# Alpha of the first nine units in ring ph, and one ScalarE sum over pc and rc

## The chip, the cores and the metric

The kernel runs on one NeuronCore of a Trainium2 chip. The metric is the time of one execution on the device in microseconds (us), as the median of several runs. The kernel before takes 537.9 us (three runs, 537.58 to 538.51).

A core has five engines that run side by side, each with its own queue of instructions in a fixed order: TensorE (PE in the profile, with PEld for the loads of its stationary operand), VectorE (DVE), ScalarE (ACT), GpSimd (POOL) and SyncE (SP), which here only starts the transfers (DMA). SBUF is the working memory with 128 partitions. PSUM takes TensorE's results; it has eight banks, each with room for 128 x 512 numbers of four bytes.

## The reference

First a gated linear attention runs over 768 steps for 4 batches, 8 heads and 48 numbers per head; then a feed-forward network with 2048 hidden numbers runs over the 3072 tokens.

```python
state = np.zeros((B, H, D, D))
for t in range(S):
    state = alpha[:, :, t, :, None] * state + einsum('bhd,bhe->bhde', k[:, :, t], v[:, :, t])
    y[:, :, t] = einsum('bhd,bhde->bhe', q[:, :, t], state)
x = y.transpose(0, 2, 1, 3).reshape(B * S, H * D)
h = x @ w_in
out = np.maximum(0.01 * h, h) @ w_out
```

B, H, S, D are 4, 8, 768, 48. All alphas lie between 0.8 and 1.

## The kernel before, in words

**Units.** The attention is cut into 24 units: 6 blocks of 128 tokens by 4 batches, block by block. Two heads lie above one another in the partitions (rows 0 to 47 and rows 64 to 111), so the 8 heads are 4 pairs. For a unit `scans` (line 330) makes `pc`, the running product of alpha along the tokens, and `rc`, its reciprocal, which is made from a reciprocal at every 16th token and one long scan from the end of the block to its start (line 342). `scaled_q` and `scaled_k` (356, 364) multiply q by `pc` and k by `rc`; `scores` (372) multiplies them on TensorE, for the even heads into one bank (`s` = 0) and for the odd heads into another (`s` = 1); `mask_scores` (381) copies both into SBUF and clears what lies after the diagonal; `k_tokens` (397) turns k back to tokens; `outputs` (407) makes the unit's output `y` (score tiles by values, line 423, and the old state by q, line 417) and the step `kv` of the state (k as tokens by values, line 434); `next_state` (447) adds it up. `sum_up` (350) sums `pc` and `rc` of the unit into `acc`; at the very end (line 646) the sums are compared with 2 to the 40th, and only if one is too large a slow exact path runs, which does not happen with these inputs.

**The output's two halves.** `y` is split into a high part `xh` (copied at line 440) and what is left, `xl`. In the first nine units TensorE subtracts `xh` in the bank of `y` itself (442) and ScalarE copies the rest (443), so `y` keeps its bank until then.

**Two ways of loading.** The first nine units (`AHEAD` = 9) are loaded with tokens in the partitions, and alpha, q and k are turned by TensorE, four transposes each, into a PSUM bank (line 302), from which VectorE works on. The later 15 units are loaded in pieces and turned by VectorE in SBUF (line 311); they take no bank for that.

**PSUM.** Ring `ph` (pool `ps_h`) has two banks, rings `a` and `b` (pool `ps_x`) three each; that is all eight. `bank()` (line 69) gives the banks of the first nine units in turn from a and b: the first call takes a, the next b, the next a, and so on. A unit makes eight calls, in the order of the program: the alpha of the next unit, its two score banks, the bank of `k_tokens`, q and k of the next unit, `y` and `kv`. Ring `ph` has the warm-up (`keep_warm`, line 188, which keeps TensorE at work with products that nobody reads), the weights 0 and 1 (lines 275 to 280), and the first product of each feed-forward item (line 515).

**Feed-forward.** The tokens of three units make a block of 384 columns, and there are 8 blocks. An item is one block and one of 16 slices of the hidden numbers: nine products into `ph` (519), the leaky maximum on ScalarE and VectorE (522 to 531), and, three items later, nine products into three banks that add up over the 16 slices (546), which are from ring b for block 0, from ring a for block 1 and from ring b for all later blocks. Blocks 0 and 1 run in turn while the weights come in: each slice arrives as 64-bit words and is made into a high and a low part by `converting` (239) on ScalarE and VectorE. From block 2 on the attention of units 9 to 23 is mixed in, a step at a time.

**Order.** The program is written down in the order of the generator `attention` (481): the scans of the next unit, then scores, mask, `k_tokens` and sum of this one, then q and k of the next, then output and state of this one. A planner that runs when the program is built follows the instructions in a model of the chip's times and gives each engine, among those whose inputs and whose bank or buffer are at hand, the one that stands first in the program; the order that comes out of it is the fixed order of each queue. `issue_after` (through `behind`, line 112) holds an instruction behind another in the same queue. `AFTER`, `BEGIN` and `STARTS` (573 to 577) are such places for the weights 0 to 2 and for the first two items.

**Buffers.** `pc` and `rc` are two tiles of [128, 4, 128] each, and each has two buffers, so the scans of a unit wait until nobody reads those of two units before. `idle`, the tile of the warm-up, is in ring ph.

Of the kernel before, what the change touches and what calls it, by code (L numbers as in the profile page):

```python
# [9 lines left out]
F32 = mybir.dt.float32  # L10
# [4 lines left out]
AF = mybir.ActivationFunctionType  # L15
# [7 lines left out]
def gated_linear_attn_ffn(ctx, tc, q, k, v, alpha, w_in, w_out, out):  # L23
    nc = tc.nc
    B, H, S, D = q.shape
    NT, DM = out.shape
    DF = w_in.shape[1]
    P = 128
    C = 128
    NC = S // C  # L30
    NP = H // 2
# [4 lines left out]
    BR = HB + D  # L36
# [3 lines left out]
    NU = len(units)  # L40
# [3 lines left out]
    cst = ctx.enter_context(tc.tile_pool(name="cst", bufs=1))  # L44
    fast = ctx.enter_context(ExitStack())
    atp = fast.enter_context(tc.tile_pool(name="atp", bufs=2))
    cvp = fast.enter_context(tc.tile_pool(name="cvp", bufs=2))
    ffp = fast.enter_context(tc.tile_pool(name="ffp", bufs=2))
    ps_h = fast.enter_context(tc.tile_pool(name="ps_h", bufs=2, space=bass.MemoryType.PSUM))
    ps_x = fast.enter_context(tc.tile_pool(name="ps_x", bufs=3, space=bass.MemoryType.PSUM))  # L50

    NL = 2, 2, 2
    NV = 3
# [4 lines left out]
    PITCH = RUN + GAP  # L58
# [10 lines left out]
    def bank(tag=None):  # L69
        if tag is None:  # L70
            tag = kinds[0]
            kinds.append(kinds.pop(0))
        return ps_x.tile([P, 512], F32, name=tag)

    def pieces(name, dtype, *shapes):

        sizes = [math.prod(shape) for shape in shapes]
        whole = cst.tile([P, sum(sizes)], dtype, name=name)
        parts = []
        for n, shape in enumerate(shapes):  # L80
            part = whole[:, sum(sizes[:n]):sum(sizes[:n + 1])]
            axes = "abc"[:len(shape)]
            if len(shape) > 1:
                part = part.rearrange(f"p ({' '.join(axes)}) -> p {' '.join(axes)}", **dict(zip(axes, shape)))
            parts.append(part)
        return parts

    ident, mask, ones, acc, seed, *rest = pieces(
        "small", F32, (P,), (C,), (1,), (2 * NU,), (NP, C), *[(NP, BR)] * B, *[(DM,)] * NV, *[(NP * PITCH,)] * sum(NL)
    )  # L90
    state, vals_sb, rest = rest[:B], rest[B:B + NV], rest[B + NV:]
    loads_sb = [[rest.pop(0) for _ in range(n)] for n in NL]
# [19 lines left out]
    def behind(*key):  # L112

        return tc.issue_after(made[key].ins) if key in made else nullcontext()
# [4 lines left out]
    def loaded(u, i):  # L119
        return places(u, i)[u % len(places(u, i))]  # L120

    def load_next(u, i):

        for n in range(u + 1, u + 3 + NS):
            if n < NU and n - len(places(n, i)) == u:
                load(n, i)

    def by_token(t):
        return t[:, 0:H * HB].rearrange("t (h d) -> t h d", h=H)
# [58 lines left out]
    def keep_warm(n):  # L188

        for _ in range(n):  # L190
            nc.tensor.matmul(idle[:, 0:C], seed[:, 0, :], seed[:, 1, :], start=True, stop=True)  # L191
# [101 lines left out]
    def banks4():  # L293
        return bank().rearrange("r (p n) -> r p n", p=NP)

    def transposed(u, i, name, **kw):

        src = loaded(u, i)
        if u < AHEAD:
            ps = banks4()  # L300
            for p in range(NP):
                last = nc.tensor.transpose(  # L302
                    ps[:, p, :], by_token(src)[:, 2 * p:2 * p + 2, :].rearrange("t h d -> t (h d)"), ident
                )
                if u == 0 and p % 2:
                    with tc.issue_after(last.ins):
                        keep_warm(2)
            return ps
        t = atp.tile([P, NP, C], F32, name=name, **kw)
        src = src.rearrange("r (p n) -> r p n", p=NP)[:, :, 0:RUN]  # L310
        nc.vector.transpose(  # L311
            t.rearrange("r p (j t) -> r p t j", t=T4),
            src.rearrange("r p (t d) -> r p t d", t=T4)[:, :, :, 0:32],
        )
        return t
# [4 lines left out]
    live, masked, sums, dense = {}, {}, {}, {}  # L320
# [6 lines left out]
    def every(t, first):  # L327
        return t.rearrange("r p (m s) -> r p m s", s=STEP)[:, :, :, first]

    def scans(u):  # L330
        aT = transposed(u, 0, "e", bufs=1)
        pc = atp.tile([P, NP, C], F32, name="pc")
        rc = atp.tile([P, NP, C], F32, name="rc")
        pe = atp.tile([P, NP, 1], F32, name="pe", bufs=3)
        for p in range(NP):
            nc.vector.tensor_tensor_scan(pc[:, p, :], aT[:, p, :], ones.broadcast_to([P, C]), 1.0, ALU.mult, ALU.mult)  # L336
        nc.vector.memset(every(aT, 0), 0.0)
        nc.vector.reciprocal(every(seed, STEP - 1), every(pc, STEP - 1))
        flat = [t.rearrange("r p t -> r (p t)") for t in (aT, seed, rc)]
        last = seed[:, NP - 1, C - 1:C]  # L340
        nc.gpsimd.tensor_copy(rc[:, NP - 1, C - 1:C], last)
        nc.vector.tensor_tensor_scan(  # L342
            flat[2][:, NP * C - 2::-1], flat[0][:, NP * C - 1:0:-1], flat[1][:, NP * C - 2::-1], last, ALU.mult, ALU.add
        )
        load_next(u, 0)
        nc.gpsimd.tensor_copy(pe, pc[:, :, C - 1:C])  # L346
        live[u] = [pc, rc, pe]
        sums[u] = pc, rc

    def sum_up(u):  # L350

        with behind("sm", u):
            for n, t in enumerate(sums.pop(u)):
                nc.scalar.activation(t, t, AF.Abs, accum_out=acc[:, 2 * u + n:2 * u + n + 1])

    def scaled_q(u):
        pc = live[u][0]
        qT = transposed(u, 1, "qs")
        load_next(u, 1)
        qs = qT if u >= AHEAD else atp.tile([P, NP, C], F32, name="qs")  # L360
        nc.vector.tensor_tensor(qs, qT, pc, ALU.mult)
        live[u].append(qs)

    def scaled_k(u):
        pc, rc, pe, qs = live[u]
        kT = transposed(u, 2, "ks")
        load_next(u, 2)
        ks = kT if u >= AHEAD else atp.tile([P, NP, C], F32, name="ks")
        made["ks", u] = nc.vector.tensor_tensor(ks, kT, rc, ALU.mult)  # L369
        live[u] = [pe, qs, ks]  # L370
# [110 lines left out]
    def attention(first, last):  # L481

        for u in range(first - 1, last):
            new, old = u + 1 < last, u >= first
            if new:
                scans(u + 1)
                yield
            if old:
                scores(u)
                yield  # L490
                mask_scores(u)
                yield
                k_tokens(u)
                sum_up(u)
                yield
            if new:
                scaled_q(u + 1)
                yield
                scaled_k(u + 1)
                yield  # L500
            if old:
                outputs(u)
                yield
                next_state(u)
                if u % UPB == UPB - 1:
                    gather(u // UPB)
                    ready.add(u // UPB)
                yield
# [71 lines left out]
    for n, _ in enumerate(st):  # L580
# [8 lines left out]
        u = AHEAD - EARLY + converted  # L589
# [4 lines left out]
        if n in STARTS:  # L594
            i, f = items[len(gs)][:2]
# [8 lines left out]
    for n in range(len(items) + LAG):  # L604
        slices = 0
        if n < len(items):
            i, f, slices, _ = items[n]
# [27 lines left out]
        for half in range(2):  # L635
# [5 lines left out]
            if half == 0 and n >= LAG:  # L641
                i, f, _, tag = items[n - LAG]
                ffn_out(i, f, gs.pop(n - LAG), tag)


    fine = cst.tile([P, 2 * NU], F32, name="fine")
    nc.vector.tensor_scalar(fine, acc, RANGE, None, ALU.is_lt)
    least = cst.tile([P, 1], F32, name="least")
    nc.vector.tensor_reduce(least, fine, mybir.AxisListType.X, ALU.min)
# [123 lines left out]
```

## Time and profile before

| | before |
|---|---|
| median of 3 runs | 537.9 us (537.58 to 538.51) |
| the profiled execution's own time | 538.98 us |
| its span in the profile | 537.2 us |
| granted TensorE clock, mean | 0.998 |
| busy PE / PEld / DVE / ACT / POOL | 98 / 94 / 69 / 44 / 11 % |
| instructions | 10028 |

Times in the profile are counted from the span's start. A row of a group names line, engine, operation, out<-in, the count, and the time of one; "idle before" is the time in which the engine had nothing to do just ahead of an instruction, and the name behind the arrow is what ended it. Ends of matmuls are modelled, so PE looks busy also where it does not run at its peak; starts are what the argument goes by. A product of four-byte numbers shows as two records, so the eight products of the scores are 16. "a" and "b" are the two rings, with the buffer's number left out.

In this profile the first nine units take the time to 66.75 us, where the first product of the feed-forward network starts. From there to 530 us TensorE works on the feed-forward network, with the attention of units 9 to 23 mixed in after 163 us.

### The profile page before, as it was taken

What the parts mean: (1) busy time and instruction counts of PE and PEld (TensorE: products, weight loads), DVE (VectorE), ACT (ScalarE), POOL (GpSimd) and SP (SyncE); (2) the same over time, 40 slices, a digit from 0 to 9 for tenths busy, and PEclk for the clock granted to TensorE, in tenths of its full rate; (3) what the DMA queues carried; (4) which work ended last, traced back from release to release, by engine and by line L of the source; (5) the groups of instructions that cost most, each with busy time, mean ns of one, the idle gap of its engine ahead of it and who ended that gap; (6) DMA issues with size and microseconds to landing.
All of it is one profiled execution on the core that took longest, in us unless ns stands there. A gap on an engine that the chain in (4) does not pass through costs nothing.

```text
span 537.2 us, 10028 instructions
## 1 busy us (share of the span) xinstructions
PE 528.6 (98%) x3807; PEld 507.3 (94%) x3807; DVE 370.8 (69%) x688; ACT 238.1 (44%) x502; POOL 59.4 (11%) x144
## 2 busy tenths in 40 slices
PE   8999999999999999999999999999999999999995
PEld 7888799999999999999999999999999999999995
DVE  7777579999999997786586685675786434333331
ACT  2667575555543544344334444335343344224331
POOL 5444210000000111101101101001010000000000
PEclk9999999999999999999999999999999999999999
DMA  9999936444835543542332432423201000001001
GB/s 146 164 205 173 231 79 133 118 119 120 194 70 147 157 97 84 103 96 72 70 88 58 114 76 49 92 54 87 70 4 35 21 26 1 22 1 45 1 1 49
DMA packets 92982, 46.64 MB, mean 87 GB/s; under 512 B 57856, under 2 KB 90112, under 8 KB 92928
## 3 DMA queue, kind: packets, MB, share of 16 engines
q1 hardware_dynamic: 92928, 45.93, 39.1%
q8 instruction: 32, 0.52, 0.5%
q14 instruction: 22, 0.18, 0.1%
HBM read 38.83 MB, written 4.72 MB: 81 GB/s over the span
## 4 chain that ended last, share of the span: by engine, by line
PE 97%; DVE 1%; issue 0%; ACT 0%; DVEq 0%
PE ph L519 38%; PE b L546 33%; PE a L546 5%; PE a L378 5%; PE a L423 3%; PE a L417 3%; PE b L423 2%; PE a L434 2%; PE a L402 2%; PE b L302 1%; PE b L378 1%; PE a L302 1%; PE ph L191 1%; PE b L417 1%; PE ph L277 1%; PE ph L279 1%
## 5 line engine op out<-in xcount | busy, mean ns | idle before, releaser
L519 PE MATMUL ph<-large,w 128*128 128x384 f32 x1152 | 225.3, 337 | 0.0
L519 PEld LDWEIGHTS ph<-large,w 128*128 128x128 f32 x1152 | 200.8, 188 | 1.1 <-PE a L423 0.2
L546 PE MATMUL b<-w,gh 128*128 128x384 f32 x672 | 168.8, 340 | 0.0
L525 DVE TENSOR_TENSOR t<-ph,t 128x384 f32<-128x384 f32 x128 | 70.2, 548 | 79.3 <-ACT t L522 79.1
L522 ACT ACTIVATE t<-ph 128x384 f32<-128x384 f32 x128 | 62.6, 490 | 135.5 <-PE ph L519 135.5
L546 PEld LDWEIGHTS b<-w,gh 128*128 128x128 f32 x672 | 119.4, 188 | 2.1 <-issue 0.4
L527 ACT CAST gh<-t 128x384 fp32r<-128x384 f32 x128 | 65.8, 514 | 108.8 <-DVE t L525 108.8
L546 PE MATMUL b<-w,gl 128*128 128x384 f32 x336 | 107.2, 335 | 0.0
L531 DVE TENSOR_TENSOR gl<-t,gh 128x384 fp32r<-128x384 f32 x128 | 70.2, 548 | 34.3 <-ACT gh L527 34.3
L546 PEld LDWEIGHTS b<-w,gl 128*128 128x128 f32 x336 | 62.6, 188 | 0.0
L389 POOL TENSOR_SCALAR_AFFINE_SELECT sm<-sm 128x512 f32<-128x512 f32 x33 | 20.6, 634 | 204.0 <-ACT sm L388 204.0
L378 PEld LDWEIGHTS a<-qs,ks 48*128 48x128 f32 x312 | 23.9, 187 | 5.5 <-issue 4.5
L378 PE MATMUL a<-qs,ks 48*128 48x128 f32 x312 | 28.6, 285 | 0.3 <-DVE ks L369 0.3
L311 DVE STREAM_TRANSPOSE ks<-small 128x512 f32<-128x512 f32 x15 | 16.6, 1117 | 14.3 <-PE a L402 14.3
L346 POOL COPY pe<-pc 128x4 f32<-128x4 f32 x24 | 5.0, 210 | 176.7 <-DVE pc L336 174.5
L395 POOL TENSOR_TENSOR small<-us,pe 48x192 f32<-48x192 f32 x40 | 20.5, 512 | 1.5
L388 ACT COPY sm<-a 128x512 f32<-128x512 f32 x24 | 14.0, 584 | 14.9 <-PE b L378 11.1
L336 DVE TENSOR_TENSOR_SCAN pc<-e,small 128x128 f32<-128x128 f32 x60 | 20.3, 397 | 0.0
L546 PE MATMUL a<-w,gh 128*128 128x384 f32 x96 | 19.3, 336 | 0.0
L342 DVE TENSOR_TENSOR_SCAN rc<-e,small 128x511 f32<-128x511 f32 x15 | 19.1, 1271 | 0.2
L423 PE MATMUL a<-sm,small 128*48 128x128 f32 x256 | 17.3, 277 | 0.0
L267 ACT CAST w<-bits 128x768 fp32r<-128x768 f32 x16 | 13.4, 841 | 8.0 <-DVE bits L264 8.0
(110 smaller groups left out, 563.9 us busy)
## 6 DMA issues: line engine op xcount, KB each, us to landing
raw<-in_moe_w_out_dram SPq DMA_DIRECT2D x16, 384.0 KB, 4.1
raw<-in_moe_w_in_dram SPq DMA_DIRECT2D x32, 144.0 KB, 4.0
out_dram<-o SPq DMA_DIRECT2D x24, 192.0 KB, 1.9
small<-in_v_dram SPq DMA_DIRECT2D x20, 192.0 KB, 3.3
small<-in_alpha_dram SPq DMA_DIRECT2D x32, 96.0 KB, 2.2
small<-in_q_dram SPq DMA_DIRECT2D x30, 96.0 KB, 2.3
small<-in_k_dram SPq DMA_DIRECT2D x30, 96.0 KB, 2.2
small<-in_alpha_dram SPq DMA_DIRECT2D x30, 80.0 KB, 2.2
```

The lines of the kernel that those rows point to most:

```text
L336: nc.vector.tensor_tensor_scan(pc[:, p, :], aT[:, p, :], ones.broadcast_to([P, C]), 1.0, ALU.mult, ALU.mult)
L378: nc.tensor.matmul(ss[s][:, p, :], ks[lo:lo + D, p, :], qs[lo:lo + D, p, :], start=True, stop=True)
L389: made["mask", u] = nc.gpsimd.affine_select(out=sm[s], in_=sm[s], compare_op=ALU.is_ge, fill=0.0, base=0, pattern=[[0, NP], [1, C]], chann ...
L395: nc.gpsimd.tensor_tensor(*scalings.pop(0))
L417: nc.tensor.matmul(y[0:BR, p, :], W[0:BR, p, :], qs[0:BR, p, :], start=p == 0, stop=False, skip_group_check=True)
L423: nc.tensor.matmul(y[lo:lo + m, p, :], V[:, c:c + m], masked[u][s][:, p, :], start=not tb and p == 0, stop=p == NP - 1, skip_group_check=True,
L519: nc.tensor.matmul(ph, w_in_of(f, wn, g), xt[:, g, :], start=n == 0, stop=n == 3 * NG - 1)
L522: put(ordered, "ACT", lambda: nc.scalar.mul(t, ph, 0.01))
L525: put(ordered, "DVE", lambda: nc.vector.tensor_tensor(t, ph, t, ALU.max))
L527: put(ordered, "ACT", lambda: nc.scalar.copy(gh, t))
L531: made["gl", i, f] = put(ordered, "DVE", lambda: nc.vector.tensor_tensor(gl, t, gh.bitcast(F32), ALU.subtract))
L546: product = nc.tensor.matmul(po[j], gt[:, js], w_out_of(f, wn), start=f == 0 and n == 0, stop=f == NF - 1 and n == 2)
```

## The change

In the first nine units the alpha of a unit is turned into a bank of ring ph and not into the next bank of a and b; q and k stay as they are. A unit so makes seven calls of `bank()`, and what had a bank of a in one unit has one of b in the next. `pc` and `rc` become the two halves of one tile with two buffers, and `sum_up` sums both in one ScalarE instruction over 1024 numbers a partition into one column of `acc`, which has 24 columns for 48; the comparison at the end is over 24 columns. The alternation for the rest of the kernel (`kinds[:] = "a"` ahead of the items) is unchanged.

```diff
-        "small", F32, (P,), (C,), (1,), (2 * NU,), (NP, C), *[(NP, BR)] * B, ...
+        "small", F32, (P,), (C,), (1,), (NU,), (NP, C), *[(NP, BR)] * B, ...
 ...
     def transposed(u, i, name, **kw):
         src = loaded(u, i)
         if u < AHEAD:
-            ps = banks4()
+            ps = banks4() if i else ps_h.tile([P, 512], F32, name="ph").rearrange("r (p n) -> r p n", p=NP)
 ...
     def scans(u):
         aT = transposed(u, 0, "e", bufs=1)
-        pc = atp.tile([P, NP, C], F32, name="pc")
-        rc = atp.tile([P, NP, C], F32, name="rc")
+        both = atp.tile([P, 2, NP, C], F32, name="pc")
+        pc, rc = both[:, 0], both[:, 1]
 ...
-        sums[u] = pc, rc
+        sums[u] = both
 
     def sum_up(u):
         with behind("sm", u):
-            for n, t in enumerate(sums.pop(u)):
-                nc.scalar.activation(t, t, AF.Abs, accum_out=acc[:, 2 * u + n:2 * u + n + 1])
+            t = sums.pop(u)
+            nc.scalar.activation(t, t, AF.Abs, accum_out=acc[:, u:u + 1])
 ...
-    fine = cst.tile([P, 2 * NU], F32, name="fine")
+    fine = cst.tile([P, NU], F32, name="fine")
```

`transposed` is called with `i` = 0 for alpha, 1 for q and 2 for k, so only alpha goes to ph.

More of the change, by code (lines that the diff above doesn't have):

```diff
@@ L88, in gated_linear_attn_ffn @@
     ident, mask, ones, acc, seed, *rest = pieces(
-        "small", F32, (P,), (C,), (1,), (2 * NU,), (NP, C), *[(NP, BR)] * B, *[(DM,)] * NV, *[(NP * PITCH,)] * sum(NL)
+        "small", F32, (P,), (C,), (1,), (NU,), (NP, C), *[(NP, BR)] * B, *[(DM,)] * NV, *[(NP * PITCH,)] * sum(NL)
     )
```

## The prediction

> **What bounds the kernel now.** I read first the page's chain of waits, to see which engine sets the end.
>
> ```profile
> PE 97%; DVE 1%; issue 0%; ACT 0%; DVEq 0%
> ```
>
> TensorE does, nearly everywhere: 97% of the chain is PE. What a change elsewhere saves counts only where it shortens PE's queue. The change touches the nine units before the feed-forward work and one ScalarE step of all 24 units, so next I cut the span into stages (window, PE busy, PEld busy, DVE busy, ACT busy, POOL busy, clock, DMA).
>
> ```profile
> 10.00:31.38 21.38, 21.04 (x257) 17.25 (x257) 17.32 (x37) 14.70 (x37) 10.38 (x25) 1.00 1.20 168
> 31.38:44.67 13.29, 13.29 (x147) 11.25 (x146) 9.51 (x21) 8.62 (x21) 6.02 (x14) 1.00 1.11 209
> 44.67:66.75 22.08, 21.66 (x191) 16.41 (x190) 14.12 (x28) 13.11 (x29) 7.04 (x12) 1.00 0.99 202
> 82.00:163.00 81.00, 81.00 (x468) 81.00 (x467) 81.00 (x132) 43.36 (x76) 0.28 (x1) 1.00 0.51 123
> ```
>
> From 10 to 66.75 us PE shows no idle time worth naming, yet the weight loads fill only 74 to 85% of it, against all of it later. So PE's queue is full but not efficient there. From 82 to 163 us PE and DVE are both full and start from the end of the first stage; what the first stage saves moves everything behind it forward. The first stage's length is therefore the question.
>
> **Where PE loses time in it.** A unit's scores are eight matrix products in two banks, `s` = 0 in rows 0 to 47, `s` = 1 in rows 64 to 111. The answers on line 378 (min/median/max ns, first and last start) for units 2 and 3:
>
> ```profile
> L378 PE MATMUL a<-qs,ks x8: 272/272/373, 20.4 to 21.3; 48*128 48x128 f32 x8
> L378 PE MATMUL b<-qs,ks x8: 272/272/373, 22.0 to 22.9; 48*128 48x128 f32 x8
> L378 PE MATMUL a<-qs,ks x8: 272/272/373, 27.1 to 27.9; 48*128 48x128 f32 x8
> L378 PE MATMUL b<-qs,ks x8: 272/272/373, 27.1 to 27.9; 48*128 48x128 f32 x8
> ```
>
> In unit 3 both halves run at once; in unit 2 one after the other, and each takes as long as the pair. Units 4 and 6 are torn in the same way; the second half of unit 6, and unit 4 in the time line of PE (start, us, what), which has the price:
>
> ```profile
> L378 PE MATMUL b<-qs,ks x8: 271/272/373, 47.1 to 48.0; 48*128 48x128 f32 x8
> 31.97 1.16 PE L378 MATMUL a<-qs,ks 48*128 48x128 f32 x8
> 33.05 0.60 PE L402 MATMUL a<-small,ks 112*128 112x112 f32 x4
> 33.58 1.16 PE L378 MATMUL b<-qs,ks 48*128 48x128 f32 x8
> ```
>
> From start to start a lone half takes 33.05 - 31.97 = 1.08 us. The order of PE's queue is fixed before the run, so this is the planner's order: it had bank a for one half and not yet bank b for the other. Such a unit also tears its products with the values apart (L434 into one bank, L423 into the other). Units 3 and 4:
>
> ```profile
> 29.79 0.32 PE L423 MATMUL b<-sm,spare 128*64 128x128 f32 x1
> 31.38 0.66 PE L302 MATMUL b<-small 128*128 128x128 f32 x4
> ...
> 35.49 0.67 PE L434 MATMUL a<-spare,ktok 128*64 128x48 f32 x16
> 36.09 0.66 PE L302 MATMUL b<-small 128*128 128x128 f32 x4
> ...
> 37.55 0.42 PE L423 MATMUL b<-sm,spare 128*48 128x128 f32 x2
> 37.90 0.66 PE L302 MATMUL b<-small 128*128 128x128 f32 x4
> 38.49 1.07 PE L423 MATMUL b<-sm,spare 128*48 128x128 f32 x14
> ```
>
> Interleaved (unit 3): 31.38 - 29.79 = 1.59 us for both. Torn (unit 4): 0.60 + 0.35 + 1.00, the last without the 0.07 us by which pieces overlap, = 1.95 us, so 0.36 more.
>
> **Why bank b is short.** The alternation gives b, in every unit, the next alpha, one score half, the next q and the output y. How long two of these hold it shows around unit 2:
>
> ```profile
> 18.21 0.32 PE L423 MATMUL b<-sm,small 128*64 128x128 f32 x1
> 19.80 0.66 PE L302 MATMUL b<-small,spare 128*128 128x128 f32 x4
> 22.43 1.28 DVE L342 TENSOR_TENSOR_SCAN rc<-b,small 128x511 f32<-128x511 f32 x1
> 24.30 0.60 ACT L443 CAST large<-b 112x512 fp32r<-112x512 f32 x1
> ```
>
> y of unit 1 from 18.21 to 24.90 is 6.7 us; alpha of unit 3 from 19.80 to the end of its backward scan at 23.71 is 3.9; together 10.6. An untorn unit needs about 5.0 us of PE, an estimate from the rows above: scores 1.08, y and kv 1.59, three transposes of 0.59 like that from 31.38 to 31.97, L402 0.53. In 5.0 us three banks offer 15, so 4.4 are left for a score half and for q, each of which is written, waits for its reader and is read. A ring so near to its limit makes the planner wait.
>
> **The change part by part.** *Alpha into ring ph.* In units 0 to 8 alpha leaves the a/b alternation: seven banks a unit instead of eight, so what took b takes a in the next unit, and y alternates. Of the 10.6 us of long holders each of the two rings then has half of y, 3.4 of its 15 us a unit, and ph has alpha, 3.9 of 10; no ring is near its limit. The number of matmuls and transposes is unchanged. If all three split units become whole: 3 x 1.08 = 3.24 us, plus 0.36 for unit 4 and the same, an estimate, for unit 2, which is torn likewise; unit 6's two pieces are each whole, so nothing there. Together 4.0 us. Bounds: 0 (the planner splits as before) to 4.0 from this alone. I take all of it, since the splits sit only where b is short, and no other ring limit is left.
>
> *What ph then meets.* Its first bank is the one the warm-up writes:
>
> ```profile
> 7.76 0.66 PE L302 MATMUL b<-small 128*128 128x128 f32 x4
> 8.25 1.95 PE L191 MATMUL ph<-small 128*128 128x128 f32 x16
> 10.40 1.35 DVE L336 TENSOR_TENSOR_SCAN pc<-b,small 128x128 f32<-128x128 f32 x4
> 48.95 1.27 DVE L342 TENSOR_TENSOR_SCAN rc<-b,small 128x511 f32<-128x511 f32 x1
> L277 PE MATMUL ph<-bits,small x8: 486/486/561, 48.7 to 59.7; 128*128 128x384 f32 x8
> ```
>
> Today alpha of unit 1 is transposed at 7.76, before the last warm-up; it will have to wait for the warm-up's end at about 10.1 or for unit 0's backward scan. That puts 0.59 us of transposes before the first scores, which began at 10.54, and DVE's scan of unit 1 some 0.4 later. Bounds 0 to 0.6; I take 0.2, since PE was idle just before the scores. Weights 0 and 1 pass through ph too (L277, from 48.7), where alpha of units 7 and 8 may hold a bank. PE would wait up to the 1.5 us from 48.7 to the end of unit 7's backward scan (48.95 + 1.27). I take 0: the first feed-forward product that needs these weights comes at 66.75 (next fence), and the units' own products can go ahead of them. Without that cover it is 1.5 for each of the two weights, most of the gain.
>
> *Banks at the end.* With 7 instead of 8 a unit, unit 8's y falls on b and the three output banks of the first feed-forward item (b) wait for its last reader. Rows:
>
> ```profile
> 66.75 3.42 PE L519 MATMUL ph<-large,w 128*128 128x384 f32 x18
> 73.88 0.86 PE L546 MATMUL b<-w,gh 128*128 128x384 f32 x4
> 75.00 0.59 ACT L443 CAST large<-a 112x512 fp32r<-112x512 f32 x1 [0.22 <-PE a L442]
> ```
>
> The third bank is wanted about 1.0 us after 73.88 and free at 75.6: 0 to 0.7 us, of which PE fills most with the next item (L519). I take 0.2.
>
> *The sums.* Two passes of 512 become one of 1024, with one accumulator read instead of two.
>
> ```profile
> L354 ACT ACTIVATE pc<-pc x24: 633/643/664, 13.1 to 448.1; 128x512 f32<-128x512 f32 x24
> 42.12 0.66 ACT L354 ACTIVATE pc<-pc 128x512 f32<-128x512 f32 x1
> 43.36 0.92 ACT L258 ACTIVATE raw<-raw 128x768 f32<-128x768 f32 x1
> 70.13 0.56 DVE L261 TENSOR_SCALAR bits<-raw 128x768 int32<-128x768 int32 x1 [7.64 <-ACT raw L258]
> ```
>
> The old pair takes 43.36 - 42.12 = 1.24 us from start to start, 0.62 each with its accumulator read, 0.02 under the 643 ns of the pass itself. From 643 at 512 to 920 at 768 is 1.08 ns an element, so 1024 takes 1.20, less the 0.02: 1.18. The saving is 0.06 us a unit (bounds, from a pass that scales with its length to one whose length is free: -0.1 to 0.6) and lies under PE's work in all units but unit 8, whose sum stands ahead of L258, on which DVE's work from 70.13 waits; I take 0.1 there. The price is a wait: both scans now write one tile, so a unit's first scan waits for the whole sum of two units before, not for its first half. The Trainium skill, "ScalarE: Activation LUTs", section "What ACT_TABLE_LOAD costs", gives 186 ns + 0.833 ns an element and an overlap of 93 ns: 1.04 us at 1024 and a saving of 0.2; its 613 ns at 512 is 5% under the row here, and the difference lies under PE by either.
>
> *Sum:* -4.0 + 0.2 + 0.2 - 0.1 = -3.7 us. The profiled execution took 538.98 (its span 537.2 and 1.8 around it), 1.1 above the median of the three runs shown, so 535.3 by its own clock and 537.9 - 3.7 = 534.2 by the median.
>
> **The rivals.** *More than that.* From 44.67 to 66.75 the weight loads leave 5.67 us free, 26%, against 15% in the stage before; at 15% it would be 2.3 us shorter. Alpha of unit 8, no longer held back by b, could be scanned in DVE's idle time (14.12 of 22.08 busy). That gives 534.2 - 2.3 = 531.9. Against it: there DVE and ScalarE convert weights between the units, and those waits stay. The Trainium skill, "Perfetto Trace Analysis", section "Identifying the Most-Contended Engine", says that matmul busy time is a bad measure of headroom and the weight loads' busy time a good one. By that rule all 11.8 us that PEld is idle from 10 to 66.75 are headroom and my sum is a third of it; the trace agrees in so far as PE shows 99% busy in a stage whose torn units cost more.
>
> *No change.* In unit 4 the second half starts right behind L402 with no idle time, and the first half already needed qs, which empties q's bank of b: on the chip nothing was waited for there. If the planner tears units for another reason than b, the splits stay or move to other units: 537.9 + 0.3 = 538.2. Against it: the whole units alternate with the torn ones, as a ring of three with four takers would.
>
> *Slower: DVE takes the next unit's scans first.* Early alpha makes the scans of unit u+2 ready as soon as the sum of unit u is done. The place is DVE's queue ahead of qs and ks of unit u+1:
>
> ```profile
> 20.56 1.36 DVE L336 TENSOR_TENSOR_SCAN pc<-b,small 128x128 f32<-128x128 f32 x4 [1.44 <-PE b L302]
> 23.74 0.19 ACT L354 ACTIVATION_READ_ACCUMULATOR rc<-rc 128x1 f32 x1
> 24.09 0.69 DVE L369 TENSOR_TENSOR ks<-a,rc 128x512 f32<-128x512 f32 x1 [0.37 <-PE a L302]
> 30.14 0.68 DVE L361 TENSOR_TENSOR qs<-b,pc 128x512 f32<-128x512 f32 x1
> ```
>
> Scans last from 20.56 to 23.71, 3.15 us. Unit 4's qs is done at 30.82 and its scores start at 31.97, so 1.15 us of delay are free and each overtaking costs 2.0. It decides where the sum ends before ks can start; in unit 3 today by 0.16 us only (23.93 against 24.09). Two such units take the gain away, three give 534.2 + 6.0 = 540.2. Against it: in whole units k and q come earlier, and the joint sum ends later than its first half did.
>
> **How the numbers follow.** The forecast has 0.5, more than that 0.15, no change 0.17, slower 0.18. I predict 534.2 us. The likeliest case alone runs from 533.8 to 536.2 (all of the 4.0 with its small costs at zero, to half of it). The range over the cases, 530.8 to 539.2, reaches 1.1 past the bigger gain, since that rival bounds its own price poorly, and to between two overtakings (538.2) and three (540.2). A measurement of this kernel tells about 0.2% from no change, 1.1 us. Faster by more than that: 0.5 + 0.15 and a little of "no change" with one split fewer, 0.68; slower 0.18; within it 0.14.
>
> **What would show it.** Right: both halves of L378 start together in units 2, 4 and 6; the stage before the first L519 ends about 3.7 us before 66.75; L336 no longer waits for PE (1.44 us at 20.56). Wrong: halves apart in any unit; L336 standing between L342 and L369 or L361 of the unit before; L277 or L302 waiting for a bank of ph; the first stage shorter but L546's first work no earlier. If the sums cost PE anything, L336 would show a wait for ACT.

## The result and the profile after

| | before | changed |
|---|---|---|
| median | 537.85 us (4 runs, 537.58 to 538.51) | 546.55 us (4 runs, 545.85 to 546.78) |
| ratio, 95% interval | | 1.0158 [1.0140, 1.0175] |
| the profiled execution | span 537.2 us | 545.85 us, span 544.1 us |
| granted TensorE clock, mean | 0.998 | 0.989 |

The change makes the kernel 8.7 us slower; 3.7 us faster was forecast. Three executions among those of the experiments below took 2861.94, 645.66 and 737.11 us, far more than the others of their kernels ("alpha alone", 64 and 32 unused bytes); the ratios leave them out, and no run here shows why.

The stages of the changed kernel (window, PE busy, PEld, DVE, ACT, POOL, clock, DMA share, GB/s):

```profile
31.38:44.67 13.29, 13.29 (x167) 12.02 (x164) 10.69 (x21) 10.06 (x20) 6.17 (x14) 1.00 1.04 230
44.67:66.75 22.08, 18.21 (x122) 13.66 (x122) 8.28 (x18) 9.01 (x17) 4.30 (x10) 0.85 0.82 192
66.75:82.00 15.25, 13.60 (x119) 12.51 (x118) 10.74 (x21) 8.84 (x16) 2.57 (x6) 0.89 0.19 52
82.00:163.00 81.00, 81.00 (x464) 80.96 (x463) 80.68 (x129) 45.31 (x77) 0.00 (x0) 1.00 0.49 126
```

Up to 44.67 us more is done than before (167 matmul records for 147, weight loads 12.02 for 11.25). Then TensorE idles 3.9 us, and its granted clock falls to 0.85 and 0.89. The answers on line 378 for units 2 and 4, which were torn before:

```profile
L378 PE MATMUL a<-qs,ks x8: 272/272/373, 21.3 to 22.1; 48*128 48x128 f32 x8
L378 PE MATMUL b<-qs,ks x8: 272/272/373, 21.3 to 22.2; 48*128 48x128 f32 x8
L378 PE MATMUL a<-qs,ks x8: 272/272/373, 30.7 to 31.6; 48*128 48x128 f32 x8
L378 PE MATMUL b<-qs,ks x8: 272/272/373, 30.7 to 31.6; 48*128 48x128 f32 x8
```

Both halves now run at once, as forecast. The time line of PE at the end of unit 6 and around unit 7, and behind it, from the kernel before, the row of line 402 in unit 6:

```profile
42.29 0.27 PE L378 MATMUL b<-qs,ks 48*128 48x128 f32 x1
42.40 0.27 PE L378 MATMUL b<-qs,ks 48*128 48x128 f32 x1
42.61 0.60 PE L402 MATMUL a<-small,ks 112*128 112x112 f32 x4
44.16 1.46 PE L277 MATMUL ph<-bits,small 128*128 128x384 f32 x4
46.69 1.46 PE L279 MATMUL ph<-pw,small 128*128 128x384 f32 x4
49.41 0.66 PE L302 MATMUL ph<-small,spare 128*128 128x128 f32 x4
54.66 0.50 PE L378 MATMUL b<-qs,ks 48*128 48x128 f32 x1 [3.87 <-DVE ks L369]
55.03 0.42 PE L378 MATMUL a<-qs,ks 48*128 48x128 f32 x1
55.24 0.42 PE L378 MATMUL a<-qs,ks 48*128 48x128 f32 x1
58.52 2.77 PE L277 MATMUL ph<-bits,small 128*128 128x384 f32 x4
```

```profile
46.35 0.60 PE L402 MATMUL a<-small,ks 112*128 112x112 f32 x4
```

Unit 6 is 46.35 - 42.61 = 3.7 us ahead, and the second half of its scores, which before stands behind this row, is done as well. Then weight 0 passes through ph. Its two sums (lines 277 to 279, one for each half of its columns) hold both banks, and alpha of unit 7 is transposed only at 49.41. What waits for it, in the time lines of ACT and DVE:

```profile
47.53 0.48 ACT L280 CAST w<-ph 128x384 fp32r<-128x384 f32 x1 [1.07 <-PE ph L279]
48.18 0.48 ACT L280 CAST w<-ph 128x384 fp32r<-128x384 f32 x1 [0.17 <-PE ph L279]
50.10 1.37 DVE L336 TENSOR_TENSOR_SCAN pc<-ph,small 128x128 f32<-128x128 f32 x4 [5.78 <-PE ph L302]
52.45 1.27 DVE L342 TENSOR_TENSOR_SCAN pc<-ph,small 128x511 f32<-128x511 f32 x1
53.82 0.69 DVE L369 TENSOR_TENSOR ks<-a,pc 128x512 f32<-128x512 f32 x1
65.72 1.36 DVE L336 TENSOR_TENSOR_SCAN pc<-ph,small 128x128 f32<-128x128 f32 x4 [8.16 <-PE ph L302]
```

The banks come free at 48.01 and 48.66 (47.53 and 48.18, each + 0.48); VectorE has by then waited most of its 5.78 us. Scan, reciprocal, backward scan and `ks` follow one another, and TensorE, whose next instructions in the fixed order are the scores that need `ks`, idles 3.87 us. When it starts again, two scores of one half lie 0.21 us apart (55.03 and 55.24; in unit 6 it was 0.11, 42.29 and 42.40) and L277 takes 2.77 us for the 1.46 of 44.16: half the clock. Unit 8 repeats it behind weight 1 (VectorE idle 8.16 us), with smaller gaps on TensorE. The longest waits of TensorE from 10 to 82 us (total, times, longest):

```profile
PE b L378 <- DVE ks L369: 3.9, 1, 3.9
PE a L378 <- DVE ks L369: 1.2, 1, 1.2
PE a L442 <- ACT large L440: 0.4, 1, 0.4
```

### The profile page after: what moved, and what is told of

The parts are those of the page before. It is cut to its first block, busy times and chain, and to the rows that moved or that the text cites. A ratio compares the mean times of both kernels' runs of the same rounds, so it can differ in the third digit from the quotient of the medians.

```text
span 544.1 us, 9975 instructions
## 1 busy us (share of the span) xinstructions
PE 531.8 (98%) x3807; PEld 511.7 (94%) x3807; DVE 374.1 (69%) x688; ACT 234.9 (43%) x454; POOL 70.9 (13%) x144
## 4 chain that ended last, share of the span: by engine, by line
PE 96%; DVE 2%; issue 0%; POOL 0%; ACT 0%; DVEq 0%
PE ph L519 38%; PE b L546 33%; PE a L546 5%; PE a L378 4%; PE a L423 4%; PE a L417 3%; PE a L434 1%; PE a L402 1%; PE ph L191 1%; PE b L423 1%; DVE pc L336 1%; PE b L378 1%; PE ph L302 1%; PE ph L277 1%; PE a L302 1%; PE b L302 1%
## 5 line engine op out<-in xcount | busy, mean ns | idle before, releaser
L519 PE MATMUL ph<-large,w 128*128 128x384 f32 x1152 | 229.8, 341 | 0.0
L519 PEld LDWEIGHTS ph<-large,w 128*128 128x128 f32 x1152 | 204.7, 189 | 1.2 <-issue 0.2
L346 POOL COPY pe<-pc 128x4 f32<-128x4 f32 x24 | 6.1, 254 | 181.1 <-DVE pc L336 179.7
L354 ACT ACTIVATE pc<-pc 128x1024 f32<-128x1024 f32 x24 | 25.7, 1071 | 0.0
L336 DVE TENSOR_TENSOR_SCAN pc<-ph,small 128x128 f32<-128x128 f32 x36 | 12.3, 402 | 17.4 <-PE ph L302 16.6
L342 DVE TENSOR_TENSOR_SCAN pc<-e,small 128x511 f32<-128x511 f32 x15 | 19.2, 1282 | 0.5
```

The source lines that it names most:

```text
L354: nc.scalar.activation(t, t, AF.Abs, accum_out=acc[:, u:u + 1])
L519: nc.tensor.matmul(ph, w_in_of(f, wn, g), xt[:, g, :], start=n == 0, stop=n == 3 * NG - 1)
```

## Experiments

The experiments ran on three chips; the medians of the kernel before were 538.4 to 538.6 us on them. Each ratio is to the kernel before on the same chip, while differences between two experiments are differences of medians and can hold some tenths of a us from one chip to another. Spacing means the mean time from the start of one feed-forward matmul record (first product, line 519; second product, line 546) to the next, from 82 to 163 us, where TensorE is never idle. The network has 2304 of these products, and each of them shows as one record, unlike the products of the scores.

**The kernel before, once more.**

> The kernel before once more, for a trace from the same chip as the following runs. Between the dense feed-forward products of 82 to 163 us the changed kernel's are 0.75% further apart than in the trace of before (175.2 against 173.9 ns). If that is the chip or the execution, this trace shows 175; if it belongs to the changed kernel, it shows 174.

538.31 us, spacing 173.89 ns (the first profile of it: 173.88). The changed kernel has 175.20. So the spacing belongs to the kernel, not to the chip or the run.

**Seven units.**

```diff
-            ps = banks4() if i else ps_h.tile(...)
+            ps = banks4() if i or u > 6 else ps_h.tile(...)
```

> The changed kernel, but only units 0 to 6 have their alpha in ring ph; those of units 7 and 8 take their turn in a and b again, so that nothing but the weights' sums stands in ph from then on. Theory (the sums of weights 0 and 1 hold both banks of ph, so alpha of units 7 and 8 comes late): the gain of the first seven units, 3.7 us, stays and the loss behind it goes: 533 to 536 us. Rival (the common tile of pc and rc makes the scans wait): as slow as the change, 545 to 547. Rival (the alternation ends on other banks and blocks the feed-forward items): in between, 540 to 545.

537.33 us, ratio 0.9984 [0.9971, 0.9997]. With alpha of units 7 and 8 back in a and b, 9.2 us of loss are gone: the loss sits in those two units. The 537.33 is above the 533 to 536 that I expected: the gain is a third of what it should be. Up to the first product of line 546 it is whole, 3.7 us (70.20 for the 73.88 in the prediction's rows):

```profile
70.20 0.50 PE L546 MATMUL b<-w,gh 128*128 128x384 f32 x2
```

Most of it is lost behind this row: the spacing is 175.19 ns for 173.89.

**The sums alone, and alpha alone.** First the common tile and its one sum with alpha as before, then alpha of all nine units in ph with two tiles and two sums.

```diff
-            ps = banks4() if i else ps_h.tile(...)
+            ps = banks4()
```

> Only the common tile and its one ScalarE sum; every alpha in the alternation of a and b as before. Theory: no change, 537 to 538.5 us, since ScalarE is not on the path. Rival (the common tile is at fault): 545 to 547.

> Only the alpha of all nine units in ring ph; pc and rc two tiles with two sums as before. Theory: all of the loss, 545 to 547 us. Rival (common tile): about 534 to 538.

The sums alone: 541.09 us, ratio 1.0052 [1.0032, 1.0072], spacing 175.17 ns. Alpha alone: 545.46 us, ratio 1.0132 [1.0109, 1.0156], spacing 173.91. So there are two losses: 7.0 us by alpha, and 2.7 by the part that I had held to be free. The second goes with the spacing: 1.3 ns x 2304 = 3.0 us.

**Is the one sum dear, or the place of the tiles?** The array of the sums is narrower by 24 numbers, 96 bytes, and every tile behind it begins lower. Three kernels separate this: the common tile and the one sum with the array left wide; the kernel before with nothing but 32 unused bytes; the kernel before with its two sums in two separate arrays, so that the tiles begin where the changed kernel has them.

The first, against the sums alone:

```diff
-        "small", F32, (P,), (C,), (1,), (NU,), (NP, C), ...
+        "small", F32, (P,), (C,), (1,), (2 * NU,), (NP, C), ...
+    acc = acc[:, 0:NU]
```

> The common tile and its one sum alone, as in the run that gave 541.09, with the array of the sums left as wide as before (72 columns, of which 36 are used), so that the tiles behind it in on-chip memory begin at the same addresses as before. Theory, the place of the tiles: the feed-forward matmuls run at 173.9 ns from one to the next as before (175.2 with the narrow array) and the time is 538.0 to 538.6. Rival, the instruction itself (one ScalarE instruction over 1024 elements, with the common tile's waits): 175.2 ns stays and the time is about 541.

The second, against the kernel before:

```diff
-        ... *[(DM,)] * NV, *[(NP * PITCH,)] * sum(NL)
+        ... *[(DM,)] * NV, *[(NP * PITCH,)] * sum(NL), (8,)
```

> The kernel before, with 32 bytes of each partition left unused behind the small tile and nothing else, so that the weights' tiles begin at a multiple of 64 bytes as in the changed kernel (32 above one before). Theory, the place: first-product matmuls from 173.2 to about 176.8 ns, second-product ones from 174.8 to 173.8, 175.2 in the mean, and 2304 of them by 1.3 ns are 3.0 us: 540.5 to 541.5. Rival, the common tile: 538.4 and 173.9 ns.

The third, against the kernel before:

```diff
-        "small", F32, (P,), (C,), (1,), (2 * NU,), (NP, C), ...
+        "small", F32, (P,), (C,), (1,), (NU,), (NP, C), ...
+    accs = acc, cst.tile([P, NU], F32, name="acc")
 ...
-                nc.scalar.activation(t, t, AF.Abs, accum_out=acc[:, 2 * u + n:2 * u + n + 1])
+                nc.scalar.activation(t, t, AF.Abs, accum_out=accs[n][:, u:u + 1])
```

> The kernel before with its two tiles and its two sums per unit, but the second sums in an array of their own that lies apart, so that the small tile is as narrow as in the changed kernel and the weights begin at the same addresses as there. Theory, the place: 175.2 ns, first-product matmuls at about 176.8, transfers at about 4.0 us, and 540.5 to 541.5, as with the common tile and its one sum (541.09). Rival, the common tile or the one instruction: 173.9 ns, transfers at 5.1 us and 538.5.

(The array has 48 columns, of which 24 are used; the first text miscounts them.) The wide array: 538.73 us, ratio 1.0006 [0.9997, 1.0015], spacing 173.88. The two sums at the changed kernel's addresses: 541.13 us, ratio 1.0049 [1.0033, 1.0064], spacing 175.17, as with the one sum. So neither the common tile nor the instruction costs anything that can be measured, and the place costs 2.6 us. The 32 bytes contradict my number, not the theory: 537.55 us, ratio 0.9986 [0.9977, 0.9994], spacing 173.33. The place alone changes the time, but a multiple of 64 bytes is not what makes it worse. Nine first products in the time lines of PE around 300 us, kernel before, 32 bytes, and two sums at the new place (there line 520, and 547 for 546):

```profile
301.44 1.72 PE L519 MATMUL ph<-large,w 128*128 128x384 f32 x9
303.00 0.52 PE L546 MATMUL b<-w,gh 128*128 128x384 f32 x2
```

```profile
301.01 1.72 PE L519 MATMUL ph<-large,w 128*128 128x384 f32 x9
302.57 0.51 PE L546 MATMUL b<-w,gh 128*128 128x384 f32 x2
```

```profile
302.58 1.75 PE L520 MATMUL ph<-large,w 128*128 128x384 f32 x9
304.16 0.51 PE L547 MATMUL b<-w,gh 128*128 128x384 f32 x2
```

From the first of the nine to the next group 1.56, 1.56 and 1.58 us. It is small in nine matmuls and 2.6 us over all.

**Alpha of seven units with two sums.** The same edit as for seven units, made to the kernel before.

> The kernel before with one edit: alpha of units 0 to 6 goes through ring ph; alpha of units 7 and 8, the tiles pc and rc and their two sums stay as before. If the 2.7 us that the single sum cost (538.42 to 541.09) is a cost on top of the gain that the seven units show, this kernel takes them off the 537.33 of the seven units: 534.6 us, range 534.0 to 535.4, which is also 3.8 less than before, the term of the prediction. If the sum's cost came from its meeting with the earlier alpha, the run stays near 537.

539.67 us (537.75 to 543.79), ratio 1.0031 [1.0013, 1.0049]: a miss. The two parts do not add. The longest waits of PE for transfers up to 82 us (total, times, longest):

```profile
PE b L302 <- DMA spare<-in_k_dram: 2.7, 1, 2.7
PE ph L302 <- DMA spare<-in_alpha_dram: 1.5, 2, 1.0
```

With the tiles at the old addresses TensorE waits for transfers once the units run earlier: 4.2 us, where 3.7 were to be gained. At the new addresses (537.33) neither wait is there. The 1.5 us for alpha come back in the next experiment, at the same addresses; the 2.7 for k do not, so the addresses alone do not explain those, and their cause is open. The loads of alpha into the spare tiles up to 45 us (KB each, median us to landing) in the kernel before, with the sums alone, and here:

```profile
spare<-in_alpha_dram SPq DMA_DIRECT2D x5, 192.0 KB, 5.1
```

```profile
spare<-in_alpha_dram SPq DMA_DIRECT2D x5, 192.0 KB, 3.7
```

```profile
spare<-in_alpha_dram SPq DMA_DIRECT2D x5, 192.0 KB, 5.3
```

So the narrower array had a good side too: alpha lands earlier, which saves the 1.5 us wherever the units run early.

**Alpha first.** With two sums and nine units in ph, the sums of weights 0 and 1 are written into the program behind the transposes of alpha of units 7 and 8 and held behind them in TensorE's queue. The conversion is cut in front of its sums, and the rest is issued when that alpha has been.

```diff
-                convert(converted)
+                parts = converting(converted)
+                if converted < SUMS:
+                    for _ in range(5):
+                        next(parts)
+                    waiting[converted] = parts
+                else:
+                    for _ in parts:
+                        pass
 ...
+        for f in list(waiting):
+            if ("tr", AHEAD - 2 + f, 0) in made:
+                with behind("tr", AHEAD - 2 + f, 0):
+                    for _ in waiting.pop(f):
+                        pass
```

> All nine units' alpha in ring ph with two sums, as in the run that gave 545.46, but the sums of weights 0 and 1 on TensorE are put behind the transposes of alpha of units 7 and 8 in program order and in TensorE's queue. Theory, the two rings' collision: alpha of unit 7 no longer waits for the weights (transposed before 42 us, not at 49.41), TensorE has no 3.9 us gap, no half clock between 54 and 62 us, and the time falls to 534 to 536. Rival, nine alphas in ph are late by their own doing (the scans, alpha's loads): about 545 again.

536.46 us, ratio 0.9959 [0.9946, 0.9971], 9.0 us less than alpha alone, and faster than both kernels; it is 0.5 above the range that I gave. Writers of ph from 40 to 72 us, of the changed kernel (from 30 us) and of this one:

```profile
L302 PE MATMUL ph<-small,spare x8: 272/273/328, 49.4 to 65.4; 128*128 128x128 f32 x8
L277 PE MATMUL ph<-bits,small x8: 484/668/847, 44.2 to 60.4; 128*128 128x384 f32 x8
```

```profile
L302 PE MATMUL ph<-small,spare x8: 270/272/329, 40.5 to 52.1; 128*128 128x128 f32 x8
L277 PE MATMUL ph<-bits,small x8: 485/486/590, 46.3 to 58.3; 128*128 128x384 f32 x8
```

Alpha of unit 7 starts at 40.5 for 49.4, the weights' sums only 2.1 later than in the changed kernel and at the full clock. The longest wait of PE that is left from 10 to 82 us is the one for alpha's transfers at the old addresses:

```profile
PE ph L302 <- DMA spare<-in_alpha_dram: 1.5, 2, 1.1
```

**The half clock by itself.** The changed kernel, with matmuls that nobody reads in the two gaps; the waits stay.

```diff
         ss = [banks4(), banks4()]
+        for _ in range({7: 15, 8: 6}.get(u, 0)):
+            nc.tensor.matmul(ss[0][:, 0, :], ident, mask, start=True, stop=True)
```

> The changed kernel with 15 matmuls (128x128, their output overwritten by the scores behind them) put ahead of the scores of unit 7 and 6 ahead of those of unit 8, so that TensorE works through most of the two gaps in which it waits for ks. Nothing else differs; the waits stay. If the half clock behind the gaps has its own price (L378 at 0.21 us instead of 0.107 from one to the next, 6.8 and 3.4 us of half clock, so 3.4 and 1.7 us of work lost), the records show the full clock from 54 to 82 us and the time falls by 3 to 5 us, to 541.5 to 543.5. If the wait for the bank is all of the loss, the time stays at 546 to 547.

541.91 us, ratio 1.0062 [1.0047, 1.0078]. The two stages:

```profile
44.67:66.75 22.08, 21.66 (x188) 17.89 (x186) 10.64 (x23) 10.35 (x20) 4.58 (x12) 1.00 0.87 212
66.75:82.00 15.25, 13.85 (x117) 13.37 (x117) 11.03 (x21) 10.47 (x19) 2.20 (x4) 1.00 0.03 9
```

More work for TensorE makes the kernel 4.6 us faster, as it keeps the clock at 1.00. In the changed kernel 0.85 over 22.08 us and 0.89 over 15.25 are (0.15 x 22.08 + 0.11 x 15.25) = 5.0 us of lost work, so this is the half clock's share. By the ratios (1.0158 to 1.0062) it is 5.2 us. The other 4.4 us (541.91 to 537.51, next run) are the waits themselves.

**Order and place.** The changed kernel with the order of "alpha first", at its own addresses, and with 128, 64 and 32 unused bytes behind the small tile.

```diff
-        ... *[(DM,)] * NV, *[(NP * PITCH,)] * sum(NL)
+        ... *[(DM,)] * NV, *[(NP * PITCH,)] * sum(NL), (32,)
```

with (16,) and (8,) in the two others.

> The changed kernel with the order alone mended: the sums of weights 0 and 1 stand behind the transposes of alpha of units 7 and 8 on TensorE. By the run with two sums (545.46 to 536.46, 9.0 less) the time falls from 546.55 to about 537.5, range 536.3 to 538.5: the transfers into the tiles, which land after about 4.0 us with this kernel's addresses (5.2 with those of before), save TensorE the 1.5 us that it waited for alpha, and the matmuls' 175.2 ns cost 3.0 again. If the place of the tiles plays no part in the transfers, TensorE waits for alpha's transfer as in the run with two sums and the time is 539 or more.

> The same with 128 bytes left unused behind the small tile, so that the weights begin where they began in the run in which the place alone was changed (32 bytes above before), while the pieces of the small tile stay where the changed kernel has them. Theory, two places with two effects: matmuls at 173.4 ns as in that run, 1.8 ns by 2304 are 4.1 us less than with 175.2: 533.4, range 532.5 to 534.5, if the transfers stay at 4.0 us; 535.5 to 537 if they go back to 5.0 with the weights' and spares' place. Rival, the place of the small tile's pieces sets the matmuls: 175.2 ns and 537.5.

> The changed kernel with the mended order, and 64 bytes left unused behind the small tile: the spare load tiles begin 64 bytes past a multiple of 256 (the changed kernel: 0, before: 96, the run with 128 unused bytes: 128). A loaded row of a head is 48 numbers, 192 bytes, and heads lie 256 bytes apart. Theory, the crossing: at 0 and at 64 the 192 bytes lie within one block of 256, at 96 and 128 they cross into the next, and that is what makes the transfers land after 5.0 to 5.3 us instead of 3.7 to 4.2; here they land after at most 4.3 and TensorE does not wait for alpha's transfer. By the Trainium skill, DMA: Bandwidth & Descriptors, section How a descriptor splits into AXI transactions, a transaction starts at a 256-byte boundary, so a piece that crosses one needs a second. Rival, only the exact multiple of 256 is fast: 5.0 us or more and a wait for alpha of about 1.5. On the matmuls no theory has a number; they have so far been 173.3 to 175.2 ns, which gives 533.4 (fast transfers, 173.3) to 537.5 (fast, 175.2).

> The same with 32 unused bytes: 32 past a multiple of 256, where 192 bytes lie within one block too. Theory, the crossing: transfers after at most 4.3 us and no wait for alpha's. Rival, only multiples of 64 bytes are fast: 5.0 us or more. Matmuls between 173.3 and 175.2 ns: 533.4 to 537.5.

The load tiles' start is given past a multiple of 256 bytes; the weights share it. The landing time is that of alpha's spare loads up to 45 us.

| unused bytes | start | us | ratio to before | spacing, ns | landing, us | wait for alpha, us |
|---|---|---|---|---|---|---|
| 0 | 0 | 537.51 | 0.9976 [0.9967, 0.9985] | 175.18 | 3.8 | none |
| 32 | 32 | 539.03 | 1.0006 [0.9996, 1.0015] | 175.39 | 4.5 | none |
| 64 | 64 | 536.14 | 0.9950 [0.9937, 0.9962] | 174.47 | 4.5 | none |
| (two sums, "alpha first") | 96 | 536.46 | 0.9959 [0.9946, 0.9971] | 173.88 | 5.3 | 1.5 |
| 128 | 128 | 536.07 | 0.9951 [0.9938, 0.9965] | 173.33 | 5.2 | 1.5 |

Without unused bytes the first product of the second kind starts 3.6 us earlier than before (70.26 for 73.88), as forecast, and the spacing takes most of that back. With 128 unused bytes the spacing is 173.33, as in the run in which the place alone was changed: so it goes with the tiles behind the small tile and not with the pieces in it, and the transfers are slow again. The 539.03 at 32 is above the range that I gave, as is its spacing. The rows of the stage 10 to 31.38 us with 64 and with 128 unused bytes, the same kernel at two places, differ in the share of the transfer engines, 1.01 for 1.25, at more bytes, 184 for 167 GB/s:

```profile
10.00:31.38 21.38, 21.17 (x277) 18.09 (x277) 18.73 (x41) 14.89 (x31) 10.80 (x25) 1.00 1.01 184
10.00:31.38 21.38, 19.71 (x258) 16.96 (x259) 17.24 (x37) 13.95 (x29) 10.16 (x24) 1.00 1.25 167
```

The wait for alpha follows the crossing: at 0, 32 and 64 the 192 bytes of a head's row lie within a block of 256, and there is no wait; at 96 and 128 they cross, and it is 1.5 us. The landing of 4.5 us is above the 4.3 that I had set, but the waits, which decide, come out as that theory says, and "only multiples of 64" and "only multiples of 256" fall. By the Trainium skill, DMA: Bandwidth & Descriptors, section How a descriptor splits into AXI transactions, a transaction that reads has to start at a 256-byte boundary, so a piece that crosses one takes two. The traces agree as far as these five places go, though here the place that moves is the one written. The spacing follows another rule, which the runs do not name; 173.3 and a fast landing did not come together at any of these addresses. Of the 1.5 us between 537.51 and 539.03, the spacing's 0.2 ns explain 0.5; the rest stays open.

## Why the prediction was wrong

**"Alpha into ring ph", -4.0: right.** No unit up to 6 is torn, unit 6 is 3.7 us ahead, and where the loss behind it is taken away 3.6 to 3.7 us remain at the first product of line 546. The splits went with alpha's place in the ring, as the account of ring b has it.

**"What ph then meets": the step that failed.** "I take 0: the first feed-forward product that needs these weights comes at 66.75 (next fence), and the units' own products can go ahead of them." They could not. The collision was seen with the wrong side waiting: I asked how long the weights would wait for alpha, which hurts nobody for long. The program has weight 0 ahead of alpha of unit 7, so the weight took both banks and alpha waited, with a chain of scan, reciprocal, backward scan and `ks` behind it that nothing covers. Mending that order alone took off 9.0 us in both versions of the sums (545.46 to 536.46, 546.55 to 537.51; by the ratios 9.3 and 9.8). The bound of 1.5 us for each weight was too small as well: it ended at the bank and left out TensorE's gap (3.87 and 1.24 us) and the clock behind it (4.6 us by the filled gap). The warm-up's part, 0.2, was too small too: the first scores start as before (10.53 for 10.54), but those of unit 1 start 0.65 us later (16.12 for 15.47; 15.48 with the sums alone).

**"The sums", -0.1: right for the instruction, wrong for the edit.** The rows of the one sum in unit 6 and its successor on ACT:

```profile
44.82 1.08 ACT L354 ACTIVATE pc<-pc 128x1024 f32<-128x1024 f32 x1
45.77 0.21 ACT L354 ACTIVATION_READ_ACCUMULATOR pc<-pc 128x1 f32 x1
45.87 0.59 ACT L443 CAST large<-a 112x512 fp32r<-112x512 f32 x1
```

45.87 - 44.82 = 1.05 us, less than my 1.18; the estimate from the figures of the Trainium skill, 1.04 (ScalarE: Activation LUTs, section What ACT_TABLE_LOAD costs), was nearer. Under TensorE's work it is worth nothing: 1.0006 with the array left wide. What I left out is that an array which shrinks by 96 bytes moves every tile behind it: 2.6 us, which go with the matmuls' spacing, less what the faster transfers give. The diff had the line; I priced its instructions only.

**"Banks at the end", 0.2:** with the order mended TensorE shows no wait at the second product up to 82 us, so 0.

**The rivals.** "More than that" did not come: the lead at the first product of line 546 was 3.6 us, and with the order mended at the changed kernel's addresses the weight loads still leave 5.3 of 22.08 us free (5.7 before), so those free microseconds were not to be had this way:

```profile
44.67:66.75 22.08, 22.08 (x182) 16.75 (x181) 11.38 (x21) 14.93 (x29) 8.79 (x14) 1.00 0.84 212
```

(The price of this rival was worked out too low: with 15% free the 16.41 us of weight loads would take 19.3 us, 2.8 less than 22.08 and not 2.3.) "No change" is out, since the splits went. "Slower" had the right sign by a mechanism that did not act: VectorE was not overtaken by early scans but waited for late ones. The sign of "wrong" in the prediction's last part, L302 waiting for a bank of ph, is the one that came, though as a late place in the fixed order: the idle time shows at the scores behind it.

**The sum put right:** from 537.85, -3.7 for the splits, +9.0 for ph, +2.6 for the place make 545.8; 546.55 was measured. The 534.2 was not reached by any version (the best median is 536.07): the earlier units meet the transfers (1.5 us) at the places 96 and 128, and the spacing is wider at 0, 32 and 64, which avoid them.

## What to carry to other kernels

When a tile moves into another ring, list who else takes banks there and in which order the program asks for them, and price the wait for both sides, above all for the one with a serial chain behind it. A gap on TensorE can cost twice: here 4.4 us for the waits and 4.6 for the clock behind them. When a small array changes its size, look at the addresses of what lies behind it, and compare with a version that only pads.

## What the runs showed of the hardware

- After a gap of 3.87 us TensorE's granted clock was half for 6.8 us, from 54.72 to 61.54. It was half again for 3.4 us, from 71.78 to 75.20, behind gaps of 0.41 and 1.24 us close together; the second of these had ended 1.1 us before. The four changes lie 6.8, 10.2 and 3.4 us apart. The Trainium skill, TensorE: Matmul & The Clock Gate, section What's actually happening, gives a window of 3413 ns: the first gap agrees, and the distances are two windows, three and one; why the shorter gaps sufficed no run here shows.
- The same matmul from the same kind of tile had a mean spacing of 175.2, 175.4, 174.5, 173.9 and 173.3 ns with the weights 0, 32, 64, 96 and 128 bytes past a multiple of 256, within 0.04 ns between kernels of one place. Over 2304 matmuls the ends are 4.7 us apart. First and second products change differently (0: 176.8 and 173.8; 96: 173.2 and 174.8; 128: 173.4 and 173.4). In the first product the streamed operand, `x`, keeps its place in all these kernels, 128 bytes past a multiple of 256, so of its operands only the weights move. In the second, nearly all tiles of `gh` and `gl` move with the weights, and which operand decides is not shown.
- Loads of alpha into the spare tiles, in 192-byte rows, landed after 3.7 to 4.5 us where the rows stayed within blocks of 256 bytes and after 5.0 to 5.3 where they crossed.
